# Amounts added to the rank of 336 operations in a kernel that plans its own order of instructions

## The chip, the cores and the metric

The kernel runs on one core of a Trainium2 chip, with its tensor engine TensorE (PE; PEld is its loading of weights), VectorE (DVE), ScalarE (ACT), GpSimd (POOL) and the SyncE queue (SP), which issues the transfers. The metric is the time of one execution on the device in microseconds (us). Each engine works through its own list of instructions in the order in which it was written; semaphores make an instruction wait for others.

## What is computed

A linear attention with decay over 4 batches, 8 heads, 768 positions and 48 values a head, and behind it two layers of 384 to 2048 to 384 over the 3072 tokens, with different activations. All data are float32; the weights of the layers arrive as 64-bit floats.

```python
def _attn_ref(r, k, v, w, u):
    for t in range(S):
        kt, vt, rt = (k[:, :, t], v[:, :, t], r[:, :, t])
        cur = np.einsum('bhd,bhe->bhde', u[None] * kt, vt)
        y[:, :, t] = np.einsum('bhd,bhde->bhe', rt, state + cur)
        state = w[None, :, :, None] * state + np.einsum('bhd,bhe->bhde', kt, vt)

def _moe_ref(x, w_in, w_out):
    h = x @ w_in
    sp = np.where(h > 20.0, h, np.log1p(np.exp(np.minimum(h, 20.0))))
    return ((h * np.tanh(sp)) @ w_out).astype(np.float32)

def _moe2_ref(x, w_in, w_out, a, b):
    h = x @ w_in
    P = a[0] + a[1] * h + a[2] * h * h + a[3] * h * h * h
    Q = 1.0 + np.abs(b[0]) * np.abs(h) + np.abs(b[1]) * h * h
    return ((P / (Q + 1e-06)) @ w_out).astype(np.float32)
```

## The kernel before

**Attention.** The 768 positions are cut into 6 chunks of 128; a chunk of one batch is a unit, 24 in all. A unit loads kraw, rraw, tkv (and, from unit 4 on, tr), multiplies k and r by powers of the decay (P_T, L674) and forms, on PE, the scores (L690), then the values (L777 and L783; L726 for units 0 and 1) and the state's increment (L752, L767). The diagonal, u·r·k, is summed in dg: for units 0 to 3 by a product on PE called dsum here (L667, with the tile uT, which two small loads of u fill), later by DVE (L683). From dg a diagonal tile am is made (diag, L707 on ACT or L704 on POOL), and the scores are written over one half of it (L712). The result y goes by a copy and two transfers (xr) into the layers' input, cut into a high part xh and a low part xl; units 0 and 1 reach xh and xl by PE and ACT alone. There are two PSUM banks named aps and three named h.

**Layers.** Each product is made of three, high by high, high by low, low by high. A block is 512 tokens in one layer; 12 blocks of 16 steps f, a step being 128 of the 2048 inner columns. A step has g1 (L872, nine matmuls of 512 columns into a bank), the activation on DVE, ACT and POOL, which ends in the high and low part gh and gl (rings of three buffers), and g2 (L948, nine matmuls into acc). The first six steps are done in halves of 256 columns. In layer 2 the bank of g1 is free again after L928; steps there go round five banks. Both layers' weights (32 tiles wr) are turned into float32 on the way: scale the high word (L62 on ACT, L64 on POOL), cut the low word (L71 on ACT, L73 on DVE), shift (L76) and sign (L80) on DVE, then copy and subtract into the high and low part w (L478, L480, L497). Five buffers wr go round.

**The order.** All operations are first collected in a plan (`Plan.add`), each with its possible engines and a planned duration. `Plan.order` gives each a rank, the longest planned way from it to the end, and then repeats: of the operations that may start, take for each engine the one of highest rank among those that start within 0.1 us of the earliest, and of these the one that starts first. This fixes each engine's list, and which engine does an operation that has a choice. Where PE would wait in the first 75 us of the plan, fillers (L941, products of zeros onto acc) are put in. The rank is set here:

```python
for op in reversed(self.ops):
    c = min(x[1] for x in op.opts) + op.lat + (0.65 + op.move if op.move else 0.0)
    op.rank = op.boost + max([c + 0.15 + x.rank - x.boost for x in op.succ + places[op]] + [t + x.rank for x, t in op.chain], default=c)
```

The small loads of a and b into cf, with two operations on them (L617, L619), stand in `setup`, among the first operations of the plan; layer 2 is the first to use cf.

Of the kernel before, what the change touches and what calls it, by code (L numbers as in the profile page):

```python
# [215 lines left out]
                    in_=x)  # L216


class Buf:


# [38 lines left out]
class Plan:  # L260
# [72 lines left out]
    def order(self):  # L333
# [11 lines left out]
        for op in reversed(self.ops):  # L345
            c = min(x[1] for x in op.opts) + op.lat + (0.65 + op.move if op.move else 0.0)
            op.rank = op.boost + max([c + 0.15 + x.rank - x.boost for x in op.succ + places[op]] + [t + x.rank for x, t in op.chain], default=c)
        free, clock = {"P": 0.0}, Clock()
        avail = [op for op in self.ops if not op.left]
        order = []  # L350
        while avail:
# [16 lines left out]
            for e, l in cand.items():  # L368
                t0 = min(x[0] for x in l)
                x = max((x for x in l if x[0] <= t0 + self.NEAR), key=lambda x: (x[1], -x[2]))  # L370
# [57 lines left out]
def fast_path(tc, nc, d):  # L428
# [40 lines left out]
    def dma(dst, src, r=(), w=(), nbytes=196608, after=(), boost=0.0, queue=SP):  # L469

        small = nbytes == 98304
        return pl.add([(queue, 0.4 if queue != SP else 0.65 if small else 0.5)],
                      lambda e: eng[e].dma_start(out=dst(), in_=src()),
                      r=r, w=w, lat=1.5 if small else 0.757, after=after, move=nbytes / 4.0e5, boost=boost)
# [39 lines left out]
    cf = fixed(cst, "cf", [128, 6])  # L514
# [50 lines left out]
    def setup():  # L565
# [16 lines left out]
        for i in range(6):  # L582
            n = 1 << i
# [28 lines left out]
                ps(), lhsT=zer(), rhs=zer()[:, None, :].to_broadcast([CH, 4, CH]), start=True, stop=True),  # L612
                r=[zer], w=[ps])
        dma(lambda: ub(), lambda: d["u"].rearrange("h e -> (h e)").partition_broadcast(CH), w=[ub])
        dma(lambda: cf()[:, 0:4], lambda: d["a"].partition_broadcast(128), w=[cf], nbytes=2000)
        dma(lambda: cf()[:, 4:6], lambda: d["b"].partition_broadcast(128), w=[cf], nbytes=2000)
        pl.add([(A, 0.1)], lambda e: nc.scalar.activation(out=cf()[:, 4:6], in_=cf()[:, 4:6], func=AF.Abs),  # L617
               w=[cf])
        pl.add([(V, 0.1)], lambda e: nc.vector.tensor_scalar(out=cf()[:, 0:4], in0=cf()[:, 0:4], scalar1=-1.0,  # L619
# [370 lines left out]
    def check_decay(after):  # L990
        f0, f1 = fixed(cst, "f0", [1, H * D]), fixed(cst, "f1", [1, H * D])
        dma(f0, lambda: d["w"].rearrange("(o h) e -> o (h e)", o=1), w=[f0], nbytes=1536)

        def fn(e):
            nc.vector.tensor_scalar(out=f1(), in0=f0(), scalar1=W_MIN, scalar2=W_MAX, op0=ALU.max, op1=ALU.min)
            nc.vector.tensor_tensor(out=f0(), in0=f0(), in1=f1(), op=ALU.is_equal)
            nc.vector.tensor_reduce(out=f1()[:, 0:1], in_=f0(), axis=AX.X, op=ALU.min)
            nc.vector.tensor_copy(fin, f1()[:, 0:1])
        return pl.add([(V, 1.7)], fn, w=[f0, f1], after=after)
# [9 lines left out]
    for s, (blk, f, half, *_) in enumerate(steps):  # L1009
        need = 0 if blk[0] else B * (blk[1] + 1) if half is None else 2 * half + 2  # L1010
        while nu < NU and nu < need:
            end = unit(nu)
            nu += 1
        if blk == (0, NC - 1) and f >= 1:
            weights(1, f - 1, [end])
        if blk == (1, 0) and f == 0:
            weights(1, NF - 1, [end])
        nxt = blocks.index(blk) + 1
        if f == 12 and nxt < len(blocks) and blocks[nxt][0] == 1:
            x2(blocks[nxt][1])  # L1020
        step(s, [end])
        if s == 3 * NF:
            check_decay([prev[1]])
    with tc.manual_schedule():
        nc.scalar.preload_act_table_set("natural_log_exp_and_others")
        pl.run()
        ok = nc.values_load(fin, min_val=0, max_val=1,
                            skip_runtime_bounds_check_because="it is a comparison's result")
# [77 lines left out]
```

## Time and profile before

| | us |
|---|---|
| median of 3 runs | 938.65 |
| lowest and highest run | 938.43 and 941.37 |
| the profiled execution | 940.34 |
| its span, first to last instruction | 938.5 |
| PE busy in the span | 914.5 |
| ACT busy | 741.6 |
| DVE busy | 679.3 |
| POOL busy | 524.5 |

Matmuls overlap in the records, since they are pipelined and their ends are modelled; how fast PE works is read from starts and counts. A row of a timeline ends, in brackets, with the time for which the engine was idle before it and what ended that. The granted clock is PE's, 1.00 being 2.4 GHz and 0.50 being 1.2 GHz.

### The profile page before, as it was taken

How to read it: one execution, taken by the hardware profiler on the slowest of the kernel's cores; microseconds unless marked ns; L12 is line 12 of the kernel's file. 1: busy time of each engine (PE TensorE's matmuls, PEld its weight loads, DVE VectorE, ACT ScalarE, POOL GpSimd, SP SyncE). 2: the span in 40 equal slices, each digit the busy share in tenths (PEclk: the TensorE clock that was granted, in tenths of full speed). 3: DMA queues.
4: the chain of work that ended last, by engine and by line, in shares of the span. 5: the costliest groups of instructions: out<-in, count | busy, mean ns of one | idle time of the engine just before them, and what ended most of it. 6: DMA issues, size and time to landing. Idle time of an engine off the chain costs nothing.

```text
span 938.5 us, 14073 instructions
## 1 busy us (share of the span) xinstructions
PE 914.5 (97%) x5072; PEld 751.6 (80%) x5072; DVE 679.3 (72%) x1025; ACT 741.6 (79%) x1303; POOL 524.5 (56%) x469
## 2 busy tenths in 40 slices
PE   8999899999999999999999999999999999999995
PEld 7789687888888788777887878888888888888884
DVE  7588986464545544549668788788887878887875
ACT  5579886777676687669798898888988978988974
POOL 4348654613800730322067698696786876876751
PEclk9899999999999999999999999999999999999998
DMA  8566435222500510343054020010100100100001
GB/s 320 168 207 199 137 119 161 76 78 74 175 1 20 183 57 1 122 160 145 1 179 159 0 68 1 7 62 0 57 12 1 57 11 1 57 1 1 34 1 37
DMA packets 37584, 73.94 MB, mean 79 GB/s; under 512 B 4609, under 2 KB 15746, under 8 KB 37506
## 3 DMA queue, kind: packets, MB, share of 16 engines
q1 hardware_dynamic: 37362, 72.70, 23.5%
q8 instruction: 41, 0.67, 0.3%
q14 instruction: 37, 0.30, 0.1%
q10 hardware_dynamic: 144, 0.26, 0.1%
HBM read 57.61 MB, written 11.01 MB: 73 GB/s over the span
## 4 chain that ended last, share of the span: by engine, by line
PE 84%; ACT 4%; DVE 4%; DMA 3%; POOL 3%; issue 1%; SPq 0%; ACTq 0%; POOLq 0%; DVEq 0%
PE acc L948 37%; PE h L872 29%; PE aps L872 8%; PE aps L690 2%; PE aps L783 2%; PE aps L777 2%; DMA wr<-in_w 2%; ACT e L891 1%; DVE wr L76 1%; DVE wr L80 1%; POOL v L910 1%; ACT gh L478 1%; PE aps L767 1%; POOL gl L497 1%; DMA rraw<-in_rT 1%
## 5 line engine op out<-in xcount | busy, mean ns | idle before, releaser
L948 PE MATMUL acc<-gh,w 128*128 128x512 f32 (+1 forms) x1188 | 390.4, 387 | 3.9 <-ACT gh L478 3.9
L872 PE MATMUL h<-xh,w 128*128 128x512 f32 (+1 forms) x960 | 315.0, 385 | 2.6 <-DVE gl L897 1.8
L891 ACT ACTIVATE e<-e 128x512 f32<-128x512 f32 (+1 forms) x408 | 242.6, 603 | 48.7 <-DVE e L887 42.0
L948 PEld LDWEIGHTS acc<-gh,w 128*128 128x128 f32 x1188 | 223.0, 189 | 50.7 <-ACT gh L478 5.7
L948 PE MATMUL acc<-gl,w 128*128 128x512 f32 (+1 forms) x594 | 229.8, 387 | 3.1 <-DVE gl L897 1.9
L872 PEld LDWEIGHTS h<-xh,w 128*128 128x128 f32 x960 | 179.0, 189 | 40.6 <-issue 2.6
L872 PE MATMUL h<-xl,w 128*128 128x512 f32 (+1 forms) x480 | 183.4, 382 | 1.0 <-DVE xl L497 1.0
L497 POOL TENSOR_TENSOR gl<-yy,gh 128x512 fp32r<-128x512 f32 x93 | 121.1, 1303 | 46.5 <-ACT gh L478 30.2
L910 POOL TENSOR_TENSOR v<-v,x 128x512 f32<-128x512 f32 x95 | 122.9, 1298 | 33.6 <-ACT v L904 19.2
L948 PEld LDWEIGHTS acc<-gl,w 128*128 128x128 f32 x594 | 112.4, 189 | 28.1 <-DVE gl L897 4.0
L887 DVE TENSOR_SCALAR e<-h 128x512 f32<-128x512 f32 (+1 forms) x102 | 66.7, 655 | 54.8 <-PE h L872 54.5
L893 DVE SCALAR_TENSOR_TENSOR h<-e,h 128x512 f32<-128x512 f32 (+1 forms) x102 | 67.1, 659 | 53.7 <-ACT e L891 53.5
L872 PEld LDWEIGHTS h<-xl,w 128*128 128x128 f32 x480 | 90.5, 189 | 18.1 <-POOL tr L678 1.4
L478 ACT ACTIVATE gh<-h 128x512 fp32r<-128x512 f32 (+1 forms) x102 | 57.7, 567 | 39.2 <-DVE h L893 37.7
L897 DVE TENSOR_TENSOR gl<-h,gh 128x512 fp32r<-128x512 f32 (+1 forms) x102 | 66.7, 655 | 27.9 <-ACT gh L478 25.3
L674 POOL TENSOR_TENSOR kraw<-kraw,P_T 128x512 f32<-128x512 f32 x20 | 26.4, 1320 | 105.2 <-DMA kraw<-in_kT 105.2
L912 ACT ACTIVATE x<-v,ceps 128x512 f32<-128x512 f32 x96 | 69.5, 724 | 14.5 <-POOL v L910 14.0
L904 ACT ACTIVATE v<-x,cf 128x512 f32<-128x512 f32 x96 | 78.1, 813 | 0.0
L872 PE MATMUL aps<-xh,w 128*128 128x512 f32 x228 | 76.0, 389 | 0.0
L922 DVE SCALAR_TENSOR_TENSOR v<-v,ceps,h 128x512 f32<-128x512 f32 x58 | 43.2, 746 | 25.2 <-ACT h L920 24.2
L902 ACT ACTIVATE x<-h 128x512 f32<-128x512 f32 x58 | 34.5, 595 | 20.3 <-PE h L872 19.9
L872 PEld LDWEIGHTS aps<-xh,w 128*128 128x128 f32 x228 | 42.8, 188 | 8.9
(136 smaller groups left out, 1362.9 us busy)
## 6 DMA issues: line engine op xcount, KB each, us to landing
wr<-in_w SPq DMA_DIRECT2D x32, 768.0 KB, 5.0
tkv<-in_tkv SPq DMA_DIRECT2D x24, 384.0 KB, 3.3
kraw<-in_kT SPq DMA_DIRECT2D x24, 256.0 KB, 2.8
rraw<-in_rT SPq DMA_DIRECT2D x24, 256.0 KB, 3.6
x<-o SPq DMA_DIRECT2D x24, 256.0 KB, 3.4
o<-x SPq DMA_DIRECT2D x24, 256.0 KB, 2.9
out_x<-o SPq DMA_DIRECT2D x17, 256.0 KB, 2.4
xr<-y SPq DMA_DIRECT2D x44, 96.0 KB, 3.3
```

The costliest lines, as they stand in the source:

```text
L478: return nc.scalar.activation(out=out, in_=x, func=AF.Copy)
L497: lambda e: eng[e].tensor_tensor(out=lo(), in0=x(), in1=hi().bitcast(F32), op=ALU.subtract),
L872: x_ = nc.tensor.matmul(h()[:, :n], lhsT=w()[:, a, m, :], rhs=x()[:, m, col:col + n], start=(i == 0), stop=(i == 8))
L887: pl.add([(V, tt(n))], lambda e: nc.vector.tensor_scalar(out=es(), in0=hp(), scalar1=20.0, scalar2=None, op0=ALU.min), r=[h], w=[e_])
L891: lambda e, func=func, kw=kw: nc.scalar.activation(out=es(), in_=es(), func=func, **kw), w=[e_])
L893: lambda e: nc.vector.scalar_tensor_tensor(out=hp(), in0=es(), scalar=-0.5, in1=hp(), op0=ALU.add, op1=ALU.mult), r=[e_], w=[h])
L897: lambda e: nc.vector.tensor_tensor(out=gls(), in0=hp(), in1=ghs().bitcast(F32), op=ALU.subtract),
L904: lambda e: nc.scalar.activation(out=v(), in_=x(), func=AF.Identity, scale=cf()[:, 5:6], bias=cf()[:, 4:5]), r=[x, cf], w=[v])
L910: lambda e: eng[e].tensor_tensor(out=v(), in0=v(), in1=x(), op=ALU.mult), r=[x], w=[v])
L912: lambda e: nc.scalar.activation(out=x(), in_=v(), func=AF.Ln, bias=ceps()), r=[v, ceps], w=[x])
L922: lambda e: nc.vector.scalar_tensor_tensor(out=v(), in0=v(), scalar=ceps(), in1=h(), op0=ALU.add, op1=ALU.mult), r=[h, ceps], w=[v])
L948: x_ = nc.tensor.matmul(ac[m]()[:, col:col + n], lhsT=w()[:, a, 3 + m, :], rhs=x()[:, :n], start=(first and i == 0 and s > 0), stop=(final ...
```

## The change

A table PRIO names 336 operations by their number in the plan, with an amount from −340 to 596 (planned us) that is added to the rank after all ranks are set. The loads of a and b and the two operations on cf move from `setup` into a function that is called after 48 of the steps, with a dependence on the last projection. No operation is added or removed but fillers, of which there are 54 in place of 32.

```diff
+PRIO = {
+    21: 17, 29: -1, 31: 384, 39: -30, 41: -150, 43: -213, 53: -152, 54: 84, 56: -56, 59: -47, 60: -2, 66: -8, 67: -5,
...
+    3373: 40, 3382: 31, 3387: 87,
+}
...
             op.rank = op.boost + max([c + 0.15 + x.rank - x.boost for x in op.succ + places[op]] + [t + x.rank for x, t in op.chain], default=c)
+        for n, x in PRIO.items():
+            self.ops[n].rank += x
...
-        dma(lambda: cf()[:, 0:4], lambda: d["a"].partition_broadcast(128), w=[cf], nbytes=2000)
-        dma(lambda: cf()[:, 4:6], lambda: d["b"].partition_broadcast(128), w=[cf], nbytes=2000)
+
+    def factors(after):
+        dma(lambda: cf()[:, 0:4], lambda: d["a"].partition_broadcast(128), w=[cf], nbytes=2000, after=after)
+        dma(lambda: cf()[:, 4:6], lambda: d["b"].partition_broadcast(128), w=[cf], nbytes=2000, after=after)
...
         if s == 3 * NF:
             check_decay([prev[1]])
+            factors([prev[1]])
```

Almost every stretch of every engine's list is written anew. Of the engines' shares, three low parts of w go from DVE to POOL, seven cuts from ACT to DVE, twelve xh from POOL to ACT and ten gh from ACT to POOL. The lines of the new kernel are higher by 39 to 42 from the class Buf on. Three places follow. In the names the number is that of the buffer.

The SP queue from its first transfer, before (wv holds the decay, in_w1 the first layer's weights):

```order
L473 DMA wv_73<-in_wT 128x4
L473 DMA uT_88<-in_u 48x4x1
L473 DMA kraw_132<-in_kT 128x512
L473 DMA rraw_134<-in_rT 128x512
L473 DMA tkv_138<-in_tkv 128x768
L473 DMA uT_88<-in_u 48x4x1
L473 DMA kraw_152<-in_kT 128x512
L473 DMA rraw_158<-in_rT 128x512
L473 DMA wr_165<-in_w1 128x1536
L473 DMA tkv_181<-in_tkv 128x768
```

and now:

```order
L512 DMA tkv_110<-in_tkv 128x768
L512 DMA wv_73<-in_wT 128x4
L512 DMA rraw_132<-in_rT 128x512
L512 DMA kraw_135<-in_kT 128x512
L512 DMA kraw_139<-in_kT 128x512
L512 DMA uT_88<-in_u 48x4x1
L512 DMA rraw_144<-in_rT 128x512
L512 DMA wr_150<-in_w1 128x1536
L512 DMA uT_88<-in_u 48x4x1
L512 DMA wr_172<-in_w1 128x1536
```

tkv goes from fifth to first, and the second load of uT from behind three large transfers to behind six, the first weight tile among them.

PE from the three zero products that open acc to the first scores, before:

```order
L937 MATMUL acc0_167<-zer_72 128x512
L937 MATMUL acc1_169<-zer_72 128x512
L937 MATMUL acc2_171<-zer_72 128x512
L667 MATMUL aps0_94<-uT_88,am_173 128x2 x4
L941 MATMUL acc0_167<-zer_72 128x512
L690 MATMUL aps1_95<-rraw_134,kraw_132 128x128
```

and now:

```order
L978 MATMUL acc0_159<-zer_72 128x512
L978 MATMUL acc1_161<-zer_72 128x512
L978 MATMUL acc2_163<-zer_72 128x512
L982 MATMUL acc0_159<-zer_72 128x512 x7
L708 MATMUL aps0_94<-uT_88,am_166 128x2 x4
L982 MATMUL acc0_159<-zer_72 128x512 x2
L731 MATMUL aps1_95<-rraw_132,kraw_135 128x128
```

Seven fillers now stand ahead of the first dsum and two behind it, where one stood behind it.

ACT from the xh of unit 1 to the activation of the first steps, before (wr_351 is the seventh weight tile, y_423 unit 2's result, e the activation):

```order
L478 ACTIVATE xh_320<-h0_96 128x3x128
L71 ACTIVATE wr_284<-wr_284 128x768
L478 ACTIVATE w_356<-wr_205 128x768
L707 ACTIVATE am_295<-dmk_85,dg_353 128x128 x4
L62 ACTIVATE wr_351<-wr_351 128x768
L478 ACTIVATE y_423<-aps1_95 128x4x128
L71 ACTIVATE wr_351<-wr_351 128x768
L891 ACTIVATE e_425<-e_425 128x256
```

and now (wr_350 is the sixth tile; the seventh, wr_472, is scaled eight rows further on):

```order
L517 ACTIVATE xh_330<-h0_96 128x3x128
L517 ACTIVATE w_389<-wr_172 128x768
L517 ACTIVATE w_406<-wr_179 128x768
L62 ACTIVATE wr_350<-wr_350 128x768
L932 ACTIVATE e_419<-e_419 128x256
L71 ACTIVATE wr_350<-wr_350 128x768
L517 ACTIVATE y_426<-aps1_95 128x4x128
L932 ACTIVATE e_419<-e_419 128x256 x3
```

The scaling in front of unit 2's y is now that of the sixth tile and no longer that of the seventh.

## Rows read from the trace of the kernel before

**Rows 1.** The page, part 1: busy us, share of the span, instructions.

```profile
PE 914.5 (97%) x5072; PEld 751.6 (80%) x5072; DVE 679.3 (72%) x1025; ACT 741.6 (79%) x1303; POOL 524.5 (56%) x469
```

**Rows 2.** Windows: from:to length, busy us by engine (instructions), PEclk, DMA share, GB/s.

```profile
0.00:31.80 31.80, 28.25 (x176) 25.23 (x176) 21.71 (x47) 19.48 (x34) 12.04 (x23) 1.00 0.78 280
31.80:58.60 26.80, 22.57 (x181) 18.65 (x179) 17.75 (x28) 13.93 (x33) 13.33 (x12) 0.87 0.59 193
58.60:95.00 36.40, 36.39 (x405) 33.62 (x406) 29.42 (x55) 31.84 (x84) 24.04 (x20) 0.95 0.64 194
95.00:115.00 20.00, 16.29 (x83) 11.90 (x82) 18.87 (x25) 17.05 (x32) 12.91 (x11) 1.00 0.36 120
115.00:420.00 305.00, 305.00 (x2026) 247.28 (x2025) 172.46 (x268) 219.31 (x398) 119.10 (x121) 1.00 0.30 93
420.00:550.00 130.00, 127.02 (x554) 103.22 (x553) 98.65 (x132) 114.54 (x189) 65.76 (x49) 1.00 0.29 105
550.00:905.00 355.00, 354.94 (x1565) 293.29 (x1565) 298.85 (x443) 306.73 (x508) 266.76 (x230) 1.00 0.06 21
905.00:938.50 33.50, 24.08 (x95) 18.43 (x93) 21.56 (x32) 18.73 (x31) 10.55 (x9) 0.91 0.07 26
```

**Rows 3.** Windows of a full DMA and of the slow clock, same columns.

```profile
7.30:20.00 12.70, 12.67 (x75) 11.93 (x75) 9.33 (x15) 9.22 (x18) 6.89 (x5) 1.00 1.02 411
38.40:45.20 6.80, 6.80 (x31) 5.54 (x32) 1.99 (x4) 4.76 (x14) 3.23 (x3) 0.50 0.26 63
58.90:62.30 3.40, 3.40 (x18) 3.32 (x16) 3.16 (x7) 3.40 (x8) 1.32 (x2) 0.50 0.65 231
922.40:925.80 3.40, 3.38 (x8) 2.73 (x9) 3.29 (x5) 1.23 (x2) 0.00 (x0) 0.51 0.00 0
```

**Rows 4.** Timeline of PE, start: start us, us, engine line op out<-in, count, idle before.

```profile
2.24 1.22 PE L611 MATMUL aps<-zer 128*128 128x512 f32 x2 [2.24 <-DVE zer L606]
...
4.54 1.48 PE L937 MATMUL acc<-zer 128*128 128x512 f32 x3
7.33 1.84 PE L667 MATMUL aps<-uT,am 128*128 128x2 f32 x8 [1.31 <-DMA uT<-in_u]
...
9.74 2.08 PE L690 MATMUL aps<-rraw,kraw 48*128 48x128 f32 x16
...
29.12 1.05 PE L667 MATMUL aps<-uT,am 128*128 128x2 f32 x8
...
30.68 1.16 PE L690 MATMUL aps<-rraw,kraw 48*128 48x128 f32 x16
31.77 0.39 PE L872 MATMUL h<-xh,w 128*128 128x256 f32 x1
```

**Rows 5.** Timeline of ACT around unit 2's y.

```profile
30.70 1.26 ACT L707 ACTIVATE am<-dmk,dg 128x128 f32<-128x128 f32 x4
36.88 0.88 ACT L62 ACTIVATE wr<-wr 128x768 f32<-128x768 f32 x1 [4.92 <-DMA wr<-in_w]
37.66 0.58 ACT L478 ACTIVATE y<-aps 128x512 f32<-128x512 f32 x1
```

**Rows 6.** Timeline of DVE behind it.

```profile
40.31 0.17 DVE L481 COPY dg<-aps 128x8 f32<-128x8 f32 x1 [4.02 <-PE aps L667]
```

**Rows 7.** Timeline of POOL and DVE, 92 to 103 us.

```profile
92.56 2.01 POOL L674 TENSOR_TENSOR kraw<-kraw,P_T 128x512 f32<-128x512 f32 x1
...
93.34 2.05 DVE L80 SCALAR_TENSOR_TENSOR wr<-wr 128x768 int32<-128x768 int32 x1
...
101.65 0.94 DVE L76 SCALAR_TENSOR_TENSOR wr<-wr 128x768 int32<-128x768 int32 x1
```

**Rows 8.** Timeline of PE and DVE at the end.

```profile
915.79 0.39 PE L872 MATMUL h<-xh,w 128*128 128x512 f32 x1
...
921.69 0.50 PE L948 MATMUL acc<-gh,w 128*128 128x512 f32 x1 [1.41 <-ACT gh L478]
...
926.59 0.75 DVE L928 SCALAR_TENSOR_TENSOR yy<-yy,cf,h 128x512 f32<-128x512 f32 x1
```

30 rows, old and new, of the table PRIO are left out of this document.

## The prediction

> **What bounds the kernel now.** I read the page's busy line first [rows 1]: TensorE (PE) is busy 914.5 of 938.5 us, so at most 24 us of idle PE can be won, plus what PE does slowly or for nothing. Then a table of stretches [rows 2], to see where those 24 us lie. From 115 to 420 and from 550 to 905 us PE is busy without a break; the second of these holds 1565 matmuls in 355 us, 0.227 us each, at full clock. An order of work can win nothing there; it can only lose. The idle time is 3.6 us before 31.8, 4.2 us from 31.8 to 58.6, 3.7 us from 95 to 115, 3.0 us from 420 to 550, and 9.4 us after 905. Beside it stands time at half clock: the granted clock is 0.50 (1.2 GHz) from 38.4 to 45.2 and from 58.9 to 62.3, and 0.51 from 922.4 to 925.8 [rows 3]; the last of them behind a PE wait of 1.41 us [rows 8]. The records begin with 1.00, but the first matmuls contradict it: scores (L690) take 2.08 us at 9.74 against 1.16 us at 30.68 [rows 4], so PE ran at 1.2 GHz until about 28 us. All that can move lies before 115 us, around 420 to 550, and at the end.
>
> **The start, up to the first projection.** Before, the first g1 (nine matmuls of 256 columns, L872) starts at 31.77 [rows 4]. From the first dsum (L667) at 7.33 on PE is nearly never idle; it is the slow clock that makes it late. The change moves two things. First, the SP queue: the second half of uT, which dsum needs, was sixth, behind four large transfers of which three (kraw, rraw, tkv, 0.92 MB) were ahead of it, and dsum was released by it at 7.33 [rows 4]. Now it stands ninth, behind tkv, two kraw, two rraw and the first weight tile (wr, 2.23 MB in all). The DMA moves 411 GB/s there [rows 3], so 1.31 MB more are 3.2 us; the first large transfer is issued about 0.9 us earlier, since tkv now goes first and not third. dsum then starts at about 9.6 us, 2.3 later. Second, 7 fillers (zero products, L941) now stand ahead of it and 17 more between there and the first g1, against 3 before. The first zero products start at 2.24, the last three at 4.54 [rows 4]; with the 7 behind them, about 0.43 us apart as three take 1.48 us, PE is dense with full-width products until about 8.5 us. If that brings the 2.4 GHz clock, dsum, scores and values take about half (1.05 us against 1.84 for dsum, 1.16 against 2.08 for scores [rows 4]) and PE stops being what binds.
>
> Next late is then ScalarE (ACT). In the new order it has, between the first dg copy and the xh of unit 1, five diag groups (1.26 us), seven passes over 768 columns (0.88 us) and eight small ones (at most 0.58 us, some 3 us together) [rows 5]: 6.3 + 6.2 + 3 = 15.5 us. From the end of dsum at 10.6 this gives 26.1, and with xl behind it about 27 us for the first g1: a gain of 4.8. If the clock stays at 1.2 GHz as long as before, PE binds as before, and the first g1 is later by the 2.3 us of dsum (fillers stand where PE waits anyway). No row shows so long a dense run this early: the eight zero products from 2.24 on did not raise the clock. Bounds −5 and +2.5; I take **−2.5**, nearer the gain, as almost twice as many now run without a gap.
>
> [...]
>
> **31.8 to 58.6 us.** In this stretch ACT reaches the scaling (L62) of the seventh weight tile, which landed only at 36.8, and waits 4.92 us; y of unit 2 stands behind it and starts at 37.66 [rows 5], though its values were ready near 35.2. The dsum of unit 3 needs the bank which y frees, so PE waits, DVE waits 4.02 us for dsum [rows 6], and the clock falls for 6.8 us. In the new order y comes after the scaling of the sixth tile, and the seventh tile's scaling comes a dozen ACT instructions later. The same order carries one more unit's values, one g1 and one g2 ahead of the last filler. What is late next is the sixth tile: its buffer is freed by the first w split on DVE, now behind xl. Nothing excludes that this wait takes back all: bounds −4.9 and 0. I take **−3**, the 2.5 us by which y was late and a bit of the slow clock.
>
> **95 to 115 us.** PE idles 3.7 us while DVE is busy 18.87 of 20 [rows 2]: the weight passes. Three low parts go from DVE to POOL, seven cuts (L71) come from ACT to DVE, so DVE's work hardly changes. But counted on the order at 0.227 us per full matmul, the g2 of steps 10 to 15 stand 7.2 to 10.9 us behind their g1 before and 9.2 to 13.7 us now, so that g2 waits less for its gh and gl. Bounds −3.7 and +2 (two passes slowed as below); I take **−2**.
>
> More work on POOL has a price: the same DVE pass (L80) takes 2.05 us at 93.34, beside a POOL product that itself takes 2.01 us, and less than half of that alone, as 0.94 us at 101.65 shows for the like-sized L76 [rows 7]. Three passes of 0.95 saved and up to three slowed by 1.1: nothing net, which is in the bounds. [...]
>
> **420 to 550 us.** 3.0 us idle [rows 2] from the second layer's weight passes on DVE and POOL. They stand in much the same places, and four of the seven cuts come to DVE here, at most 0.94 us each [rows 7]. Bounds −3 and +3; I take **0**.
>
> **The full stretches.** Nothing to win. From 115 to 420 the shortest way from a g1 to its g2 is 7.2 us at six places, against 8.2 before: bounds 0 and +1, in the next term's value. From 550 to 905 the new order runs in bursts: up to eight projections open at once (four or five before), five g1 in a row, then five g2. Counted on the order at 0.227 us per matmul, the shortest time from the end of a g1 to the g1 five later, which takes over its bank, is 12.2 us at six places, against 14.3 before. What must fit in there is the chain from the last g1 matmul to the end of L928: from 916.0, when the last one (915.79) has streamed, to 927.3, 11.3 us [rows 8]. It fits with 0.9 us to spare. In the other direction slack grows: the shortest time from g1 to its g2 is 10.2 us against 8.2. Bounds 0 and +5 with both stretches; I take **+1**.
>
> **The tail.** After the last g1 (its last matmul starts at 915.79) five g2 follow to the end, and PE waits at 921.69 for gh and falls to the slow clock [rows 3, 8]. Now six g2 follow, so the last g1 is one group, 9 × 0.227 = 2.0 us, earlier, and the chain behind it, which sets the end, starts earlier by as much. Bounds −3 (with the slow clock) and +0.5 (more of the other steps' work queued on DVE); I take **−2**.
>
> Moving the two loads of a and b to the middle takes two issues of 0.4 us out of a queue that waits on buffers there: nothing.
>
> **Sum:** −2.5 − 3 − 2 + 0 + 1 − 2 = **−8.5**. The profiled run took 940.34 us, 938.5 of it span; 940.34 − 8.5 = 931.8. The median of the runs is 938.65, 1.7 lower, so I forecast **930.1**.
>
> **The rivals.**
> *More of the same:* nearly every term at its good end, −5 − 4.9 − 3.7 − 1 + 0 − 3 = −17.6, 921. For it: PE's idle and slow time before 115 us is larger still. Against it: fillers and DVE's load remain. Chance 0.13.
>
> *DVE swallows the start:* from 45 to 115 us DVE is nearly full, so a start that is earlier only queues its work sooner; the first three terms are nil and 0 + 1 − 2 = −1 stays, 937.6. For it: 18.87 of 20 busy. Against: DVE is idle 9 of the 26.8 us from 31.8 to 58.6 [rows 2]. Chance 0.16.
>
> *The clock falls in the start:* fillers run out at 8.5 us, uT lands at 9.6, PE rests, and PE stays at 1.2 GHz: +2.5, the next term only −1, the others −3: −1.5, 937.1. It decides by whether dsum starts at full speed. Chance 0.07.
>
> *Bursts starve PE (slower):* in the second layer a chain that meets two slowed DVE passes (+1.1 each) takes 13.5 us and misses the 12.2 us at six places by 1.3, 8 us; and at eight places the three gh/gl buffers must come round in 4.1 us (two such places before), one slowed pass each, 8 us more. With +16 in place of +1 the sum is +6.5, 945.1. It decides from the point where a chain takes over 12.2 us. For it: DVE 84% and ACT 86% busy there, where order is all that keeps PE fed. Against: no stall at all in 355 us now, and more slack from g1 to g2. Chance 0.14.
>
> **How the numbers follow.** Forecast 0.50. A measurement of this kernel tells about 0.3% (2.8 us) from no change, so faster means below 935.8 and slower above 941.5. The forecast gives 0.46 faster, 0.03 same, 0.01 slower; the large gain 0.13 faster; DVE 0.04, 0.11, 0.01; the clock 0.02, 0.04, 0.01; bursts 0.01, 0.02, 0.11. Together 0.66, 0.20, 0.14. The range, 919.5 to 941.5, leaves out the bursts above it and a part of the large gain below it, some 0.18.
>
> **What would show it.** dsum at about 9.6 us and scores in 1.1 us right after; the first g1 at 27 to 30; no 4.9 us ACT wait ahead of y; no PE clock fall near 38; PE idle under 2 us from 95 to 115; 550 to 905 still idle-free; six g2 after the last g1 and no slow stretch at the end. The forecast is wrong if PE shows idle gaps of a microsecond in the second layer, or if the first g1 starts after 32.

## The result, and the profile after

| | before | after |
|---|---|---|
| median of 4 runs each, side by side, us | 940.01 | 927.93 |
| lowest and highest | 938.43, 942.63 | 926.85, 930.53 |
| the profiled execution, and its span | 940.34, 938.5 | 926.85, 925.1 |

The new kernel takes 0.9873 of the old one's time, 95% interval 0.9838 to 0.9907: 12 us less, 9 to 15. The forecast was 8.5 less. By the bounds that the prediction set itself (faster below 935.8) that is faster, and it is inside the range; but the parts of the sum are another matter, as its first term has the wrong sign and three others are too small.

The busy line of after (us, share of the span, instructions), against [rows 1]:

```profile
PE 908.6 (98%) x5094; PEld 750.6 (81%) x5094; DVE 678.9 (73%) x1028; ACT 735.3 (79%) x1310; POOL 525.1 (57%) x468
```

The same stretches as in [rows 2], of after (from and to, length, busy us and instructions by engine, granted clock, DMA share, GB/s):

```profile
0.00:31.80 31.80, 26.08 (x140) 22.44 (x141) 17.38 (x41) 14.64 (x30) 6.27 (x18) 0.73 0.68 226
31.80:58.60 26.80, 25.67 (x244) 22.26 (x244) 22.85 (x34) 20.80 (x47) 15.59 (x12) 1.00 0.76 258
58.60:95.00 36.40, 34.98 (x395) 31.16 (x394) 34.81 (x59) 30.91 (x82) 21.59 (x20) 1.00 0.61 184
95.00:115.00 20.00, 19.22 (x142) 15.73 (x141) 13.03 (x22) 16.92 (x35) 15.70 (x16) 1.00 0.45 152
115.00:420.00 305.00, 304.47 (x1986) 246.75 (x1985) 181.25 (x272) 217.44 (x400) 124.97 (x121) 1.00 0.28 88
420.00:550.00 130.00, 130.00 (x576) 107.71 (x575) 103.97 (x145) 116.23 (x197) 69.68 (x51) 1.00 0.33 116
550.00:905.00 355.00, 355.00 (x1567) 293.93 (x1566) 297.12 (x448) 310.89 (x510) 265.49 (x230) 1.00 0.06 21
905.00:925.10 20.10, 13.18 (x59) 10.58 (x57) 8.47 (x13) 7.51 (x13) 5.79 (x5) 0.90 0.13 44
```

Before 31.8 us PE now does fewer matmuls (140, of which 18 are fillers, against 176 with 3 fillers in [rows 2]); from there to 115 us more, and at full clock throughout; from 420 to 550 us there are 576 in place of 554; and at the end the stretch is short. The full stretch from 550 to 905 us is as full as it was.

To give this a size in us, each matmul start of a trace is counted with what its shape takes at full speed (0.2267 us for 512 columns, 0.1195 for 256, and so on; fillers count nothing), and the sum is compared with that of before at the same time. The result is the **lead**: how many us of PE's work a kernel is ahead. At the end it is the difference of the spans. The rows under after are experiments, told below.

| lead over before, us, at | 31.8 | 58.6 | 95 | 115 | 420 | 560 | 900 | end |
|---|---|---|---|---|---|---|---|---|
| after | -4.5 | +1.6 | -0.6 | +3.7 | +2.9 | +8.2 | +8.2 | +13.4 |
| e8: start of before, then after | -0.1 | +4.4 | +4.0 | +9.4 | +9.1 | +14.3 | +14.3 | +19.6 |
| e9: after from 31.8 to 386 alone | -1.2 | +1.8 | +1.2 | +6.1 | +5.0 | +5.0 | +4.8 | +5.7 |
| e12: after up to 386 | -4.6 | +1.2 | -0.2 | +5.6 | +4.1 | +5.0 | +5.0 | +5.4 |
| e6: after from 386 to 564 alone | -1.2 | +0.6 | +1.4 | +3.4 | +1.6 | +6.8 | +6.8 | +7.0 |
| e5: after from 870 alone | 0.0 | -0.1 | -0.2 | +0.5 | -1.4 | -0.2 | -0.9 | +4.0 |

A lead is of one execution each. Where e5 and e6 still run the order of before, they differ by 3 us at 115; e8 and e9, whose lists are the same up to 386 us, differ by 3.3 at 115 and 4.1 at 420. So a number here is good to 3 or 4 us in what it brings from the first 115 us, and to a few tenths in what it gains later from one column to the next.

The start of after, PE's timeline (start, us, engine, line, operation, tiles, shapes, count, idle time before and what ended it); dsum is L708, scores L731, g1 L913 and fillers L982:

```profile
5.78 1.97 PE L982 MATMUL acc<-zer 128*128 128x512 f32 x7
11.27 1.02 PE L708 MATMUL aps<-uT,am 128*128 128x2 f32 x8 [3.52 <-DMA uT<-in_u]
12.80 1.91 PE L731 MATMUL aps<-rraw,kraw 48*128 48x128 f32 x16
17.09 1.86 PE L708 MATMUL h<-uT,am 128*128 128x2 f32 x8
20.37 2.08 PE L731 MATMUL h<-rraw,kraw 48*128 48x128 f32 x16
37.45 0.28 PE L913 MATMUL h<-xh,w 128*128 128x256 f32 x1
```

With the fillers PE is at full speed when dsum comes: it takes 1.02 us, against 1.84 in [rows 4]. It is so (0.95 to 1.02) in all seven traces with these seven fillers, and in two of the seven without them (e6 and e11). But dsum waits 3.52 us for uT, and the second dsum (17.09) and scores (20.37) run at the slow speed again. The first g1 starts at 37.45, 5.7 us later than before. The chain of waits of after has this piece there (start, us, what):

```profile
4.58 6.44 DMA uT<-in_u
11.02 0.25 issue
11.27 1.02 PE aps L708 x8
```

In the trace of before the same load is issued at 3.15 and lands 4.04 us later. Other first inputs are late too, as DVE's timeline of after shows (the same two instructions start at 2.49 and 5.40 before):

```profile
4.26 0.17 DVE L613 TENSOR_SCALAR wv<-wv 128x4 f32<-128x4 f32 x1 [2.12 <-DMA wv<-in_wT]
7.57 0.69 DVE L702 TENSOR_TENSOR am<-kraw,rraw 128x512 f32<-128x512 f32 x1 [2.15 <-DMA kraw<-in_kT]
```

And at the end, where [rows 8] show the wait of 1.41 us, the last g1 of after and the six g2 behind it (54 matmuls) follow one another without a gap, and the chain of waits of after ends in PE alone:

```profile
903.90 2.04 PE h L913 x9
905.94 12.25 PE acc L989 x54
918.19 0.02 issue
918.22 0.60 ACT o L517
```

The last matmul (PE's timeline):

```profile
917.79 0.39 PE L989 MATMUL acc<-gh,w 128*128 128x512 f32 x1
```

### The profile page after: what moved, and what is told of

It is laid out like the page before. It is cut to its first block, busy times and chain, and to the rows that moved or that the text cites. A ratio compares the mean times of both kernels' runs of the same rounds, so it can differ in the third digit from the quotient of the medians.

```text
span 925.1 us, 14144 instructions
## 1 busy us (share of the span) xinstructions
PE 908.6 (98%) x5094; PEld 750.6 (81%) x5094; DVE 678.9 (73%) x1028; ACT 735.3 (79%) x1310; POOL 525.1 (57%) x468
## 4 chain that ended last, share of the span: by engine, by line
PE 91%; DVE 4%; DMA 2%; ACT 2%; issue 1%; POOL 0%; SPq 0%; POOLq 0%; ACTq 0%; DVEq 0%
PE acc L989 41%; PE h L913 32%; PE aps L913 8%; PE aps L731 2%; PE aps L824 2%; PE aps L818 2%; PE acc L982 1%; DVE wr L80 1%; DVE wr L76 1%; DMA uT<-in_u 1%; DMA wr<-in_w 1%; DVE w L536 1%; ACT e L932 1%; PE aps L808 1%; ACT am L748 0%
## 5 line engine op out<-in xcount | busy, mean ns | idle before, releaser
L989 PE MATMUL acc<-gh,w 128*128 128x512 f32 (+1 forms) x1188 | 378.0, 385 | 0.7 <-ACT gh L517 0.7
L913 PE MATMUL h<-xh,w 128*128 128x512 f32 (+1 forms) x960 | 307.0, 384 | 1.8 <-DVE gl L938 1.1
L932 ACT ACTIVATE e<-e 128x512 f32<-128x512 f32 (+1 forms) x408 | 238.1, 602 | 59.1 <-DVE e L928 53.2
L913 PEld LDWEIGHTS h<-xh,w 128*128 128x128 f32 x960 | 178.6, 188 | 39.1 <-DVE gl L938 1.1
L913 PE MATMUL h<-xl,w 128*128 128x512 f32 (+1 forms) x480 | 183.4, 382 | 0.4 <-DVE xl L536 0.4
L913 PEld LDWEIGHTS h<-xl,w 128*128 128x128 f32 x480 | 90.3, 188 | 17.5 <-DVE xl L536 0.6
L517 ACT ACTIVATE gh<-h 128x512 fp32r<-128x512 f32 (+1 forms) x99 | 55.7, 564 | 31.4 <-DVE h L934 31.0
L913 PE MATMUL aps<-xh,w 128*128 128x512 f32 x228 | 75.1, 390 | 0.0
L715 POOL TENSOR_TENSOR kraw<-kraw,P_T 128x512 f32<-128x512 f32 x19 | 26.7, 1406 | 55.3 <-DMA kraw<-in_kT 55.3
L955 DVE TENSOR_TENSOR yy<-yy,h 128x512 f32<-128x512 f32 x58 | 39.7, 686 | 20.9 <-ACT yy L948 18.8
L913 PEld LDWEIGHTS aps<-xh,w 128*128 128x128 f32 x228 | 42.8, 188 | 8.8
```

Source lines behind the costliest of these rows:

```text
L517: return nc.scalar.activation(out=out, in_=x, func=AF.Copy)
L913: x_ = nc.tensor.matmul(h()[:, :n], lhsT=w()[:, a, m, :], rhs=x()[:, m, col:col + n], start=(i == 0), stop=(i == 8))
L932: lambda e, func=func, kw=kw: nc.scalar.activation(out=es(), in_=es(), func=func, **kw), w=[e_])
L989: x_ = nc.tensor.matmul(ac[m]()[:, col:col + n], lhsT=w()[:, a, 3 + m, :], rhs=x()[:, :n], start=(first and i == 0 and s > 0), stop=(final ...
```

## The experiments

The order that the planner makes is a list of pairs, operation and engine, and each engine's queue is what that list holds for it. For the experiments the lists of before and after are written out, and edited or spliced: the first part of one, then all that is not yet done in the order of the other. So nothing but the order differs, and an operation stays on the engine that its list gives it. In all of them the loads of a and b stand in the middle, as in the new kernel. The splices are put where both lists have done nearly the same operations.

| | what it runs | median, us | ratio to before, 95% interval |
|---|---|---|---|
| e1 | after, uT first | 923.48 | 0.9825 (0.9808 to 0.9843) |
| e2 | after, SP queue of before at the start | 924.64 | 0.9836 (0.9819 to 0.9853) |
| e10 | e2, and dg ahead of the first scaling on ACT | 922.67 | 0.9823 (0.9803 to 0.9843) |
| e3 | before, SP queue of after at the start | 943.06 | 1.0034 (1.0012 to 1.0056) |
| e4 | before, seven fillers ahead of dsum | 940.32 | 1.0008 (0.9991 to 1.0026) |
| e8 | before up to the first g1, then after | 920.66 | 0.9820 (0.9794 to 0.9845) |
| e11 | e8 without its later fillers | 924.65 | 0.9831 (0.9810 to 0.9852) |
| e9 | after from 31.8 to 386 us alone | 932.75 | 0.9920 (0.9897 to 0.9942) |
| e12 | after up to 386 us | 936.84 | 0.9986 (0.9972 to 1.0000) |
| e7 | after up to 126 us | 947.42 | 1.0091 (1.0069 to 1.0113) |
| e6 | after from 386 to 564 us alone | 936.69 | 0.9967 (0.9951 to 0.9983) |
| e5 | after from 870 us alone | 936.35 | 0.9966 (0.9950 to 0.9982) |

The median of before, in the four groups of runs, was 938.7 to 940.6. One per cent is 9.4 us.

Moving the loads of a and b has a price where the order of before runs in the middle. In the traces of e3, e4, e5 and e6 (and of e7) ACT and DVE wait there for a and b, and PE then has a wait of 1.15 to 1.45 us between 327 and 338 us, which neither before nor after has, nor a kernel that runs the new order up to 386 us. In e4 (ACT's timeline, then PE's; L715 is an operation on cf):

```profile
323.11 0.20 ACT L715 ACTIVATE cf<-cf 128x2 f32<-128x2 f32 x1 [3.01 <-DMA cf<-in_b]
330.42 1.08 PE L875 MATMUL aps<-rraw,st 48*48 48x128 f32 x16 [1.15 <-DVE am L810]
```

The chain of waits of e4 runs from the one to the other. From start to start PE loses 1.2 to 1.5 us there. No run makes this move alone, so this is read from traces; by it the times of e3 to e6 lie that much higher against before than their own edits make them.

### The start: a late uT

e1, the SP queue:

```diff
-tkv, wv, rraw, kraw, kraw, uT, rraw, wr, uT, wr
+wv, uT, uT, tkv, rraw, kraw, kraw, rraw, wr, wr
```

> The new order with one edit: wv and both halves of uT are the first three transfers of the SP queue, and every other instruction stands where the new order has it. My theory of the start: the late uT (it lands at 11.2 us, dsum waits 3.52 us for it, and the granted clock falls to 0.50 at 13.0) is what makes the first g1 5.7 us later than before. Then dsum is released by DVE's first product instead, at about 8.4 us, the clock stays full, the first g1 starts at 30 to 32 and the time is 4 to 6 us under that of the new order (922 to 924). Rival: ScalarE and VectorE bind the start whatever PE does; dsum is earlier, the first g1 stays within a microsecond of 37.4, and the time stays within 1.5 us of 927.9.

e2, the SP queue:

```diff
-tkv, wv, rraw, kraw, kraw, uT, rraw, wr, uT, wr
+wv, uT, kraw, rraw, tkv, uT, kraw, rraw, wr, wr
```

> The new order with one edit: the first nine transfers of the SP queue stand in the sequence that they had before (wv, uT, kraw, rraw, tkv, uT, kraw, rraw, the first weight tile), all else as in the new order. Theory of the late uT: dsum starts at 7.3 to 7.5 us, right behind the fillers and at full clock, scores takes 1.2 us, the first g1 starts at 27 to 31, and the time is 6 to 9 us under the new order's, 919 to 922. Rival (ScalarE and VectorE bind the start): the first g1 stays at 36 to 37.5 and the time within 1.5 us of 927.9. A second rival: the start gains as said, but VectorE, which is nearly full from 58 to 115 us, gives it back there; the first g1 is at 27 to 31 and the time at 926 to 929.

In both (and in e10) POOL's clearing of uT also stands first in its queue again, as it did before; in after it comes behind the constants.

Measured: 923.48 and 924.64, that is 4.4 and 3.3 us under after by the medians. All five runs of e2 and five of the six of e1 are faster than the fastest of after (926.85), though the intervals touch. The late uT, with what goes late beside it, is a cause, in the size expected for e1 and short of it for e2. dsum starts at 8.46 and 8.38, yet the first g1 comes only at 39.0 and 35.9 in the profiled executions (e1's is, at 928.17, its slowest by far). So the start has a second fault. It shows in e2's timelines, first of PE and then of ACT (scores is L788 here, dg<-aps L574, the scaling L62):

```profile
8.38 0.95 PE L765 MATMUL aps<-uT,am 128*128 128x2 f32 x8
9.83 0.48 PE L788 MATMUL aps<-rraw,kraw 48*128 48x128 f32 x2
11.63 1.86 PE L788 MATMUL aps<-rraw,kraw 48*128 48x128 f32 x13 [1.32 <-ACT dg L574]
```

```profile
10.61 0.92 ACT L62 ACTIVATE wr<-wr 128x768 f32<-128x768 f32 x1 [8.51 <-DMA wr<-in_w]
11.42 0.16 ACT L574 ACTIVATE dg<-aps 128x8 f32<-128x8 f32 x1
```

The copy of dg, which DVE makes at 9.21 before, is ACT's now and stands behind a scaling that waits for the first weight tile. PE waits 1.32 us for it, and is slow again by 13 us (L728 at 13.38 takes 2.37 us for 14 matmuls, where e4 has 1.47 for 16).

e3, the SP queue in the order of before:

```diff
-wv, uT, kraw, rraw, tkv, uT, kraw, rraw, wr, tkv
+tkv, wv, rraw, kraw, kraw, uT, rraw, wr, uT, tkv
```

> The order of before with one edit: the first nine transfers of the SP queue stand in the new order's sequence (tkv, wv, rraw, kraw, kraw, uT, rraw, weight tile, uT); the loads of a and b stand in the middle, as in the new order. Theory of the late uT: dsum starts at 11 to 11.5 us in place of 7.3, the first g1 at 35 to 37 in place of 31.8, and the time is 3 to 5 us over that of before, 943 to 945. Rival (later stages have slack that takes it up): the first g1 is as late, but the time is within 1.5 us of 940.

Measured: 3.2 us over before (1.1 to 5.3), dsum at 10.75, the first g1 at 35.85, near what the theory said. But part of the 3.2 is the wait for a and b: counted as in the table of leads, e3 is 1.0 to 1.4 us behind before from 115 to 320 us, and 2.7 at 420. So in the order of before the late transfers cost some 1 to 2 us, less than in the new one; and the interval of the time, less 1.5, reaches below zero.

e4, PE's queue in the order of before:

```diff
 three zero products onto acc
+seven zero products onto acc
 dsum of the first unit
```

> The order of before with one edit: seven more zero products stand ahead of the first dsum, as in the new order; the SP queue is that of before (with the loads of a and b in the middle). This is what my prediction took the first term for. Theory: the clock is full from about 6.2 us on, dsum takes 1.05 us and scores 1.16 in place of 1.84 and 2.08, the first g1 starts at 27 to 29 and the time is 2 to 4 us under that of before, 936 to 938. Rival: the clock falls again soon, since PE has gaps between the small stages, and the first g1 is within a microsecond of 31.8, the time within 1.5 us of 940. Second rival: the start gains, and VectorE or ScalarE takes it back before 115 us: first g1 at 27 to 29, time 939 to 941.

Measured: 0.8 us over before (0.8 under to 2.4 over); the first g1 at 31.68 against 31.77. The first rival holds. PE in e4:

```profile
8.39 0.95 PE L765 MATMUL aps<-uT,am 128*128 128x2 f32 x8
9.61 1.16 PE L788 MATMUL aps<-rraw,kraw 48*128 48x128 f32 x16
12.01 1.05 PE L765 MATMUL h<-uT,am 128*128 128x2 f32 x8
15.86 2.07 PE L788 MATMUL h<-rraw,kraw 48*128 48x128 f32 x14 [2.35 <-ACT P_t L574]
```

dsum and scores run at full speed, just as my prediction wanted, and nothing that can be measured comes of it, with or without the 1.2 us for a and b: PE then waits 2.35 us for ACT's copy of P_t, is slow again, and what stands behind starts when it did before.

e10, ACT's queue in e2:

```diff
-scaling of the first weight tile (L62)
 dg<-aps of the first unit
+scaling of the first weight tile (L62)
```

> The new order with the first nine transfers of the SP queue in their old sequence, and one more edit: ScalarE's copy dg<-aps of the first unit stands ahead of its first scaling of a weight tile (L62), behind which it waits until the tile lands at 10.6 us. Theory: scores no longer waits 1.32 us for dg at 11.6 us, the whole chain of the start moves by 1.5 to 2.1 us, and the time is 1 to 2.5 us under that of the queue's edit alone, 922 to 923.6. Rival: the clock, which has fallen by 13 us either way, or VectorE's first product of unit 1 at 11.1 us sets the pace; dg is earlier, the second dsum is not, and the time stays at 924 to 925.5.

Measured: 922.67, where the theory put it, and the first g1 at 35.15 against 35.94; but the intervals of e2 and e10 overlap, so that the 2 us between them are likely and not shown. Nor is this the whole rest of the start: the first g1 of e8 (below) starts at 31.91. In the chain of waits of e10 17 fillers stand between dsum and the first g1 and take 6.6 us of it; in the timeline of before it is 3 fillers. No run leaves these out, so it is open whether they only fill waits or hold back what stands behind them.

e8, the list of operations (131 pairs up to the first g1):

```diff
-AFTER
+BEFORE[:131], then AFTER without what is done
```

> The order of before up to the first g1 (about 31.8 us, at a place where the two orders have done the same work but for five operations), the new order for the rest: the late uT, the late wv and kraw and the early fillers are all gone. Theory (the start's loss of 4.6 us adds to the rest): the first g1 at 31.8, and the time 4 to 6 us under the new order's, 922 to 924, as with uT first. Rival: an earlier start meets a VectorE or a DMA queue that is full from 45 to 115 us, the lead at 115 us stays 3 to 4 us, and the time within 1.5 us of 927.9.

Measured: 920.66, 7.3 us under after by the medians, more than expected, and 5.0 by the ratios to before, as expected. From 115 us on its lead is 5.7 to 6.2 us over that of after, and nothing takes it back: DVE, which is busy 10 of the 10 us from 45 to 55 there, does not swallow it. The whole start, then, costs 5 to 7 us, of which the queue explains 3.3 to 4.4; the rest has no run of its own but e10.

e11, PE's queue in e8:

```diff
-30 zero products behind the first g1
```

> The order of before up to the first g1 and the new order for the rest, without any of the zero products (fillers, 30 of them) behind the first g1. Theory: fillers stand where PE waits anyway, and what they are worth is the clock, which stays full from 31.8 to 60 us with them; without them it falls to 0.50 at least once between 36 and 62 us, and the time is 2 to 5 us over that of the same kernel with them (920.7), 923 to 926. Rival: PE's real work keeps the clock up by itself and the fillers only delay what stands behind them: 919 to 921.

Measured: 924.65. The windows of e11 behind the first g1:

```profile
41.00:45.00 4.00, 4.00 (x32) 3.65 (x31) 1.74 (x4) 2.99 (x9) 3.55 (x4) 0.70 0.74 287
55.00:60.00 5.00, 2.96 (x23) 2.37 (x23) 5.00 (x9) 2.86 (x7) 1.29 (x1) 0.71 0.53 188
```

and of e8:

```profile
41.00:45.00 4.00, 4.00 (x53) 3.73 (x52) 4.00 (x6) 3.60 (x8) 3.79 (x3) 1.00 0.62 200
55.00:60.00 5.00, 5.00 (x64) 4.19 (x63) 4.87 (x11) 5.00 (x15) 0.36 (x1) 1.00 0.70 211
```

With the fillers the granted clock is 1.00 in every window of e8 from 31.8 to 70 us; in e11, without them, it falls around 40 and again around 60 (0.84 from 36 to 41 us, 0.70 to 45, 1.00 to 55, 0.71 to 60, 0.61 to 65). The medians differ by 4 us, as the theory had it, but the intervals overlap, and the first g1 of e11 started 2.1 us later than that of e8, though the two lists are the same up to there. A trace with the fillers and a start like that of e11 is at hand: e9 (next) runs the list of e8 up to 386 us, and its first g1 started at 34.41, that of e11 at 34.03. Counted alike, the lead of e11 is 2.5 at 58.6 us and 4.8 at 420; that of e9 is 1.8 and 5.0. So the clock fell without the fillers, but of these two traces the one without them is not behind by more than 0.2 us at 420; the 4 us between e8 and e11 are not shown to be the fillers'.

### The stages by themselves

e9:

```diff
-AFTER
+BEFORE[:131], then AFTER up to its place 1494, then BEFORE
```

> The order of before up to the first g1, the new order from there to about 386 us, the order of before for the rest: the new order of the stretch from 31.8 us on alone, without its start, its middle and its tail. If the stages add up, it is worth what is left when the middle (5.2) and the tail (4.9) are taken from the 20 us that the kernel with the start of before and the new order behind it won: about 9 to 10 us, a time of 930 to 932, where my prediction had 3 + 2 - a part of 1 = 4 to 5 us, a time of 935 to 936. Rival, as the seam at 126 us showed: at the seam a tile is not there in time, PE waits several us once, and the time is 935 or more with one long PE gap near 386 us; then only the lead at 380 us tells (9 us by the theory).

Measured: 7.5 us under before (5.5 to 9.7), 932.75. The seam costs one gap of 1.1 us at 403 us. The lead at 420 us is 5.0, less than the 9 expected and shown by e8, which runs the same list up to there; this execution, the slowest of e9's six, had its first g1 at 34.41 against 31.91 in e8 (the last section says where that comes from).

e12:

```diff
-AFTER
+AFTER[:1494], then BEFORE
```

> The new order up to about 386 us, the order of before for the rest: the seam at 126 us, at which PE waited 6 us for a bank, is avoided by one at which the two orders differ in six operations only. Theory: the new order's lead at 420 us, 2.9 us in its own trace, is real and kept: 935.5 to 938.5; with the kernel that has the start of before and the same seam (932.75) this prices the start, 3 to 6 us lost. Rival: the lead is a matter of the start's clock in one execution, and the first part is worth nothing: 939 to 941.

Measured: 1.3 us under before (0.0 to 2.6); by the medians 1.9. With e9 and the same seam this prices the start: 0.9986 less 0.9920 is 0.66%, 6.2 us lost; by the medians, each against its own before, 4.8.

e7:

```diff
-AFTER
+AFTER[:650], then BEFORE
```

> The new order up to about 126 us, the order of before for the rest. If the stages add up, what is left is the new order's lead of 3.7 us at 115 us (4.6 lost up to 31.8, some 8.3 won from there to 115): 935 to 937. Rival (the lead at 115 us is given back, since the stretch from 115 to 420 us cannot start earlier than its weights allow): 938.5 to 940.

Measured: 8.6 us over before, neither of the two. The lead at 115 us was 3.3, as expected, and the seam threw it away, PE's timeline of e7:

```profile
150.43 0.39 PE L1046 MATMUL acc<-gh,w 128*128 128x512 f32 x1
156.45 0.80 PE L788 MATMUL aps<-rraw,kraw 48*128 48x128 f32 x4 [5.64 <-ACT y L574]
```

The two lists differ in 14 operations there, and the bank that scores needs is, by the releaser shown, held by a y that ACT makes late; the wait for a and b comes on top. The run says nothing about the stage. e12 took its place.

e6:

```diff
-BEFORE
+BEFORE[:1472], then AFTER up to its place 2128, then BEFORE
```

> The order of before up to about 386 us and from 564 us on, the new order between. My prediction gave this stretch nothing, with 3.0 us of idle PE as the most that it could win. Theory: idle time tells too little, since a matmul's record goes on while PE waits to start the next; 553 matmuls in 130 us at 0.2267 us each leave 4.6 us in which none started, and the new order (575 matmuls) wins nearly all of it: 934 to 936. Rival: at most the idle time, 3.0 us, or part of it: 937 to 940.

Measured: 3.1 us under before (1.6 to 4.6); by the medians 3.9. The lead grows by 5.2 us from 420 to 560, as in after (5.3) and e8 (5.2). The time and the lead agree if the 1.5 us for a and b, which fall before 420 us, are taken off the time: 4.6. Two windows of before and then the same two of e6:

```profile
420.00:440.00 20.00, 18.61 (x82) 14.85 (x81) 18.23 (x24) 19.08 (x31) 5.65 (x5) 1.00 0.54 219
540.00:560.00 20.00, 18.66 (x79) 14.25 (x78) 18.39 (x29) 19.69 (x34) 19.83 (x19) 1.00 0.24 79
```

```profile
420.00:440.00 20.00, 20.00 (x90) 16.58 (x89) 16.34 (x23) 19.43 (x33) 4.95 (x5) 1.00 0.79 310
540.00:560.00 20.00, 20.00 (x89) 16.38 (x88) 17.07 (x26) 19.19 (x33) 19.92 (x16) 1.00 0.06 15
```

Before is idle 1.39 and 1.34 us in them, but does 8 and 10 matmuls fewer, which is 1.8 and 2.3 us. Matmul records overlap: the record of the last one before a wait goes on for 0.39 us, though the next could start after 0.23. So each wait costs PE more than the idle time shown.

e5:

```diff
-BEFORE
+BEFORE[:3273], then AFTER
```

> The order of before up to about 870 us, the new order for the rest (six g2 behind the last g1 in place of five); the loads of a and b stand in the middle. What is a tail worth? My prediction said 2.0 us, one group of nine matmuls by which the chain behind the last g1 starts earlier. A count of the traces says more: the new order has done 8.2 us more of useful PE work at 900 us and ends 13.4 us earlier, so that 4.9 to 5.2 us come from the tail, which is what the matmul starts behind 900 us lose before (4.6 us). Theory by the count: no PE gap behind 905 us and a time of 934 to 936. Rival (the prediction's term): 937 to 938.5.

Measured: 3.2 us under before (1.7 to 4.7); by the medians 4.2. The lead grows by 4.9 us from 900 us to the end, as in after (5.2) and e8 (5.3). The prediction's term of 2 lies inside the interval of the time, but the trace speaks for the count, and so does the time without the 1.5 us for a and b: 4.7 under before. The last matmul of before:

```profile
930.56 0.39 PE L948 MATMUL acc<-gh,w 128*128 128x512 f32 x1
```

From 905 to there are 25.6 us with 95 matmuls [rows 2], 21.5 us at 0.2267 each: at least 4.0 lost (the first one or two of a count began before 905). In after it is 59 from 905 to 917.8, 13.4 us of work in 12.8: nothing lost.

**The parts together:** start +6.2 (e12 less e9), 31.8 to 386 us -7.5, middle -3.1, tail -3.2 are -7.6 us by the ratios and -10 by the medians (e9 stands in the first two and falls out of the sum); without the 1.5 us for a and b in each of the last two it is -10.6 and -13. The change took 12 (9 to 15). Each splice has its own seam to pay for, and each of the four numbers is good to 1.5 or 2.5, so that the parts agree with the whole within what was measured, and no better.

## Why the prediction was right, and where it was not

That the forecast of 8.5 us came near is luck: a loss that it took for a gain stood against gains that it took too small. By the sign that it had set itself for being wrong, a first g1 after 32, its account of the start was wrong (37.45).

**The start: -2.5 forecast, 5 to 7 lost; the step that failed is "uT, then the clock, then ACT's 15.5 us".** Four things in it were wrong. *The landing:* I took 1.31 MB at 411 GB/s, dsum at 9.6; it came at 11.27. The rate of [rows 3] was not reached so early. In the windows of after from 5 to 9 us the DMA moved 230 and then 370 GB/s:

```profile
5.00:7.00 2.00, 2.00 (x8) 1.59 (x7) 0.42 (x5) 0.00 (x0) 0.00 (x0) 1.00 0.82 230
7.00:9.00 2.00, 0.75 (x4) 0.27 (x2) 1.44 (x7) 0.00 (x0) 0.00 (x0) 1.00 1.02 370
```

The transfer of 0.8 KB took 6.44 us behind the large ones. In the traces of before and after this small load takes the longer to land the more bytes stand ahead of it in the queue: the two of before took 1.9 us behind 2 KB and 4.04 us behind 0.92 MB, the two of after 5.2 us behind 1.18 MB and 6.44 us behind 2.23 MB. *The clock:* I asked whether fillers could raise it, and with them it was up (dsum 1.02 us); the question was whether PE would then be kept busy. In e4 all of that happened with an early uT and the gain was nil, since the second scores waits 2.35 us for P_t. The rival "the clock falls in the start" named the place, but its own sign, dsum at the slow speed, did not come, and its +2.5 was half of what the start cost or less. *The bound of 2.5:* it held only dsum's lateness. wv and kraw are late as well, and in e2 dg on ACT is behind a scaling; I had put ACT's work down as a sum of durations (15.5 us), without looking at what its first instruction waits for. *The path:* the sum itself was good, ACT is busy 15.1 us from its first dg at 12.33 to the end of the xh of unit 1 at 35.40; but the other 8 us it waits for PE and DVE, 5.6 of them for PE's values (L767):

```profile
26.07 0.87 ACT L517 ACTIVATE tr<-aps 128x384 f32<-128x384 f32 x1 [3.62 <-PE aps L767]
32.46 0.85 ACT L517 ACTIVATE tr<-h 128x384 f32<-128x384 f32 x1 [1.98 <-PE h L767]
```

So the start is a chain that goes to and fro between PE and ACT, and not the work of one engine.

The gain of 4.8 us that the prediction worked out for a fast PE did not come: in e4 dsum (0.95 us) and the first scores (1.16 us) are fast, and the first g1 starts at 31.68, against 31.77. The 2.4 and 1.2 GHz of the prediction can be had from starts in the trace of before as columns per ns, an estimate that counts a column as one period: at full speed matmuls of 512 columns start 0.2267 us apart (550 to 905 us) and those of 256 columns 0.12 (32.0 to 33.9 us), so that 256 columns more take 0.107 us, 2.4 per ns; at a granted clock of 0.50 it is 0.427 us (923.9 to 925.6 us) and 0.214 (60.4 to 62.1 us), 1.2 per ns.

**31.8 to 58.6 us: -3 forecast, within -4.9 and 0.** The mechanism was right: ACT's timeline of after has no wait of L62 ahead of y, PE's clock is 1.00 over the whole stretch, and y starts 3.1 us behind the first g1 where it was 5.9 [rows 4, 5]:

```profile
39.71 0.91 ACT L71 ACTIVATE wr<-wr 128x768 int32<-128x768 uint16 x1
40.51 0.59 ACT L517 ACTIVATE y<-aps 128x512 f32<-128x512 f32 x1
```

In e8, which starts as before did, the lead grows by 4.5 there; in after by 6.1, of which a part makes up for the start.

**58.6 to 95 us: no term in the forecast, 2.2 lost in after, 0.4 in e8.** Why is open.

**95 to 115 us: -2 forecast, -4.3 in after and -5.4 in e8.** The bound of 3.7 was PE's idle time. Before, six waits there lost about 5 us when counted from start to start. What the three low parts on POOL cost, no run tells apart.

**420 to 550 us: 0 forecast, -5.2.** The step that failed is "they stand in much the same places": they do, but the little that moved took all its waits away (from 554 matmuls to 576). And the bound of 3 was idle time again.

**The full stretches: +1 forecast, about +0.5 measured** (the lead falls by 0.8 from 115 to 420 us in after and by 0.3 in e8, and stays level from 560 to 900). The bursts did not starve PE: 355.00 of 355 us busy. Counting the shortest way round the banks (12.2 us) against the chain (11.3 us) held.

**The tail: -2 forecast, about -5.** "One group earlier" was counted; the waits and the slow clock of [rows 3, 8], which go away with it (the granted clock of after is 1.00 from 900 us to its last matmul at 917.8), were put into the bound only, and that ended at 3. Nor does the chain behind the last g1 set the end any more: in after it is PE, with the 54 matmuls shown above.

**The loads of a and b: nothing forecast.** In the new order that holds, as PE has no wait for them in after; in the order of before the same move costs 1.2 to 1.5 us.

**The rivals.** DVE did not swallow the start: e8 keeps what it gains. "More of the same" was right for all terms but the first: e8 comes out at 920.7, where that rival had 921. It, e1, e2, e10 and e11 all beat both kernels by their medians; which of them is best, the intervals don't tell.

## What to carry to other kernels

The most that a stretch can give back is the time in it less its matmuls at their full-speed distance from start to start; idle time between records that overlap was 23 to 41% too small here. A small load that the first product needs goes to the head of its queue, ahead of large ones (0.8 KB took 1.9 us behind 2 KB here and 6.44 us behind 2.23 MB), and before dummy work is counted on to keep the clock up, the next thing that PE waits for behind it has to be found. A change of order is best priced stage by stage, by splicing the two orders where they have done the same work, a seam must be looked at for a wait of its own, and an edit that all the splices share (here the loads of a and b) needs a run by itself.

## What was not expected of the hardware

The clock's rise in the start is not a matter of the order alone. e6 runs the order of before up to 386 us, without the early fillers, and its PE was at full speed from 7.7 us on and slow again in L728 (2.63 us against 1.47 in e4):

```profile
7.73 1.02 PE L765 MATMUL aps<-uT,am 128*128 128x2 f32 x8 [1.71 <-DMA uT<-in_u]
9.03 1.16 PE L788 MATMUL aps<-rraw,kraw 48*128 48x128 f32 x16
10.02 2.63 PE L728 MATMUL h<-idn,P_T 48*128 48x48 f32 x16
```

In the profiled execution of before the same dsum took 1.84 us [rows 4]. Being fast early did not help: the first g1 of e6 started at 34.68, against 31.77. The traces say where these 2.9 us arise. At 27.4 us e6 is 0.2 us behind before. Then PE of before gets to full speed, and that of e6 is still slow at 35.9 us (matmuls of 256 columns start 0.21 us apart, against 0.12 in before). The third dsum in e6, e9, e11 and e8 (in before it is the 1.05 us at 29.12 in [rows 4]):

```profile
29.81 1.87 PE L765 MATMUL aps<-uT,am 128*128 128x2 f32 x8
29.54 1.87 PE L765 MATMUL aps<-uT,am 128*128 128x2 f32 x8
29.16 1.87 PE L764 MATMUL aps<-uT,am 128*128 128x2 f32 x8
29.26 1.05 PE L765 MATMUL aps<-uT,am 128*128 128x2 f32 x8
```

Of the seven executions that run the start of before with its SP queue, four have the fast one (before, e4 with its seven more fillers, e5, e8) and their first g1 at 31.7 to 31.9; three have the slow one (e6, e9, e11) and it comes at 34.0 to 34.7. So one order has two starts, some 2.5 us apart at the first g1, and which one an execution gets does not go by its clock at 7.7 us (e9 was slow there, e6 and e11 fast). What decides it stays open. A lead at 31.8 or 58.6 us is to be read with this in mind.
